# Funnel attention followed by a multiplicative FFN: early keys, queries and w3 transposed on TensorE instead of by DMA, weight loads spread between pairs, FFN work issued per matmul under a time budget

## The chip, the cores and the metric

The kernel runs on one core of one Trainium2 chip. The metric is the device time of one execution in microseconds (us). The span of a profiled run is about 1.8 us shorter than its time.

## The reference

```python
# q, k, v: (8 batches, 8 heads, 1152, 64); x: (4608, 512)
q_pool = q.reshape(B, H, S // 2, 2, D).mean(axis=3)              # 576 queries
scores = (1 / sqrt(D)) * q_pool @ k.T                            # 576 x 1152 per head
attn   = exp(scores - max) / sum
x      = (attn @ v) laid out as (B*576, 8*64)
a, b   = x @ w1, x @ w2                                          # 512 -> 1024
out    = ((a * b) @ w3) @ w_out                                  # 1024 -> 1024 -> 512
```

The kernel computes T = w3 @ w_out once, so that the last line is (a * b) @ T.

## The kernel before

The 64 heads are handled as 32 pairs of heads. For each pair a flat string of 9 key blocks x 576 queries = 5184 columns of scores runs through TensorE, and the strings of all pairs are cut into chunks of 512 columns, 324 in all. One iteration of the main loop handles two chunks: scores on TensorE into PSUM, the memory that takes its results (`psc`), the exponential on ScalarE into SBUF, the memory that its operands come from (`er`), the attention matmuls for what is ready (`po`, one accumulator for the whole pair), and FFN matmuls as filler so that TensorE does not stand while ScalarE works. There are 162 iterations, and 5184 / 1024 = 5.06 of them belong to a pair.

Scores need keys and queries transposed (`kT`, `qT`). Before, the DMA does this for every pair, and also for w3. `kst` (loaded keys) has 4 buffers, so the load for pair P + 4 waits until VectorE has copied the keys of pair P into `kc`.

```python
def prep(P):                                        # cut: the rows of the first two pairs
    kc = ab.tile([128, NJ, 2, D], FP16, tag="kc", bufs=2, name="kc")
    nc.vector.tensor_copy(out=kc..., in_=kst.pop(P))
    kT[P] = ab.tile([128, NJ, 128], FP16, tag="kT", bufs=3, name="kT")
    nc.sync.dma_start_transpose(out=kT[P], in_=kc.rearrange("p j u d -> p (j u d)"))
    ...                                             # qp = sum of neighbouring queries, VectorE
    qT[P] = ab.tile([128, NJ, 64], FP16, tag="qT", bufs=3, name="qT")
    nc.sync.dma_start_transpose(
        out=qT[P], in_=qps[pp][o:o + 64].rearrange("p c u d -> p (c u d)"))
    nc.vector.tensor_copy(out=vts[P % 4][:, :, :, 0:D], in_=vst.pop(P))

def scores(c):
    t = psum.tile([128, 2, CH], FP32, tag="psc", bufs=2, name="psc")
    ...                                             # matmuls: 64 rows, up to 512 columns
def expo(c):
    nc.scalar.activation(out=er[:, :, r:r + CH], in_=psc.pop(c), func=AF.Exp, ...)

def w3_transpose():                                 # once, at iteration 3
    for i in range(2):
        nc.sync.dma_start_transpose(out=w3T[:, 4 * i:4 * i + 4]..., in_=w3h[i]...)

def gen_ffn(t, tail):                               # filler: one yield = 4 matmuls of 512 columns
    ...
            pa = bank("pa", tail and ft % 2)
            for mc in range(NC):
                nc.tensor.matmul(pa, w1sb[...], xT[:, mc, t0:t0 + 512], ...)
            ...
            yield

load_k(0); load_q(0); load_v(0); prep(0)
load_k(1); load_q(1); load_v(1); prep(1)
load(2); load(3); load_w(); load_w12()
...
for it in range(NIT):
    if it == 3: w3_transpose()
    if it == 6: filler.append(gen_T())
    ...
    scores(2 * it);     expo(2 * it)
    scores(2 * it + 1); expo(2 * it + 1)
    if prepped < NP and it * 2 * CH >= (prepped - 2) * PAIR + 2 * CH:
        prep(prepped); prepped += 1                 # two pairs ahead of use
        if loaded < NP: load(loaded); loaded += 1
    credit = min(credit + 24 / 20.0, 2.4)           # filler pieces per iteration
    while (SQ * (nextJ + 1) - 1) // CH <= 2 * it - 1:
        attend(nextJ); nextJ += 1
        if nextJ % NJ == 0: fill(1)
    fill(3)
...                                                 # the last FFN units after the loop
```

The softmax here doesn't subtract the row's maximum and nothing guards it: scores larger than these inputs give would overflow.

Of the kernel before, what the change touches and what calls it, by code (L numbers as in the profile page):

```python
# [8 lines left out]
FP16 = mybir.dt.float16  # L9
AF = mybir.ActivationFunctionType  # L10
ALU = mybir.AluOpType
# [12 lines left out]
def kernel(  # L24
# [17 lines left out]
    NF = dff // 128  # L42
    NP = B * H // 2
    SCL = 16.0
    SCALE = 0.5 * float(D) ** -0.5

    const = ctx.enter_context(tc.tile_pool(name="const", bufs=1))
# [11 lines left out]
    wosb = const.tile([128, NF, dm], FP16)  # L59
    er = const.tile([128, 2, RING], FP16)  # L60
    vts = [const.tile([128, 2, NJ, VW], FP16, name=f"vt{i}") for i in range(4)]

    ctx.enter_context(tc.manual_schedule())

# [29 lines left out]
    def load(P):  # L94
        if P < NP:
            load_k(P)
            load_q(P)
            load_v(P)

    def prep(P):  # L100

        kc = ab.tile([128, NJ, 2, D], FP16, tag="kc", bufs=2, name="kc")
        nc.vector.tensor_copy(out=kc.rearrange("p j u d -> p u j d"), in_=kst.pop(P))  # L103
        kT[P] = ab.tile([128, NJ, 128], FP16, tag="kT", bufs=3, name="kT")
        nc.sync.dma_start_transpose(out=kT[P], in_=kc.rearrange("p j u d -> p (j u d)"))
        pp, o = P // 2, 64 * (P % 2)
        if P == 0:
            qps[pp] = ab.tile([128, NJ, 2, D], FP16, tag="qp", bufs=2, name="qp")
            rows = [slice(0, 64)]
        elif P == 1:  # L110
            rows = [slice(64, 128)]
        elif P % 2 == 0:
            qps[pp] = ab.tile([128, NJ, 2, D], FP16, tag="qp", bufs=2, name="qp")
            rows = [slice(0, 128)]
        else:
            rows = []
        for r in rows:
            src = qst[pp][r].rearrange("p u (c two) d -> p u c two d", two=2)
            nc.vector.tensor_tensor(
                out=qps[pp][r].rearrange("p c u d -> p u c d"),  # L120
                in0=src[:, :, :, 0, :], in1=src[:, :, :, 1, :], op=ALU.add)
        qT[P] = ab.tile([128, NJ, 64], FP16, tag="qT", bufs=3, name="qT")
        nc.sync.dma_start_transpose(
            out=qT[P], in_=qps[pp][o:o + 64].rearrange("p c u d -> p (c u d)"))
        nc.vector.tensor_copy(out=vts[P % 4][:, :, :, 0:D], in_=vst.pop(P))


    psc = {}
# [22 lines left out]

    po = {}

    def attend(J):

        P, j = divmod(J, NJ)
        if j == 0:
            po[P] = psum.tile([128, 2, 512], FP32, tag="po", bufs=1, name="po")
        r = (J * SQ) % RING
        for u in range(2):  # L160
            for i in range(5):
                f = 128 * i if i < 4 else SQ - 128
                nc.tensor.matmul(  # L163
                    po[P][:, u, VW * i:VW * i + D + 1],
                    er[:, u, r + f:r + f + 128],
                    vts[P % 4][:, u, j, 0:D + 1],
                    start=(j == 0 and i == 0), stop=(j == NJ - 1 and i == 4),
                    skip_group_check=True)
        if j < NJ - 1:
            return  # L170
        acc = po.pop(P)[:, :, 0:5 * VW].rearrange("p u (i w) -> p u i w", w=VW)
        rz = ab.tile([128, 2, 5, 1], FP32, tag="rz", bufs=2, name="rz")
        nc.vector.reciprocal(out=rz, in_=acc[:, :, :, D:D + 1])  # L173
        xn = ab.tile([128, 5, 2, D], FP16, tag="xn", bufs=3, name="xn")
        nc.vector.tensor_tensor(  # L175
            out=xn.rearrange("p i u d -> p u i d"), in0=acc[:, :, :, 0:D],
            in1=rz.to_broadcast([128, 2, 5, D]), op=ALU.mult)
        b, hp = divmod(P, 4)
        n0 = b * SQ
        nc.sync.dma_start_transpose(  # L180
            out=xT[:, hp, n0:n0 + 512].rearrange("p (i r) -> p i r", r=128),
            in_=xn[:, 0:4].rearrange("p i u d -> p (i u d)"))
        nc.sync.dma_start_transpose(
            out=xT[:, hp, n0 + 512:n0 + SQ].rearrange("p (i r) -> p i r", r=64),
            in_=xn[64:128, 4].rearrange("p u d -> p (u d)"))
# [1 line left out]

    w3h = []

    def load_w():  # L190
        for i in range(2):
            t = ffp.tile([128, 4, dff], FP16, tag="g", name="w3h")
            nc.gpsimd.dma_start(
                out=t, in_=moe_w3.rearrange("(c p) f -> p c f", p=128)[:, 4 * i:4 * i + 4])
            w3h.append(t)
        nc.gpsimd.dma_start(out=wosb, in_=moe_w_out.rearrange("(c p) f -> p c f", p=128))

    def load_w12():
        nc.gpsimd.dma_start(out=w1sb, in_=moe_w1.rearrange("(c p) f -> p c f", p=128))
        nc.gpsimd.dma_start(out=w2sb, in_=moe_w2.rearrange("(c p) f -> p c f", p=128))  # L200

    def w3_transpose():
        for i in range(2):
            nc.sync.dma_start_transpose(
                out=w3T[:, 4 * i:4 * i + 4].rearrange("p c a f -> p (c a) f"),
                in_=w3h[i].rearrange("p c f -> p (c f)"))

    def bank(pre, wide):
        if not wide:
            return psum.tile([128, 512], FP32, tag="ff", bufs=2, name=pre)  # L210
        return psum.tile([128, 2, 512], FP32, tag="psc", bufs=2, name=pre)[:, 0, :]

    def gen_T():

        for c in range(NF):
            pt = bank("pT", False)
            for a in range(NF):
                nc.tensor.matmul(pt, w3T[:, c, a, :], wosb[:, a, :],  # L218
                                 start=(a == 0), stop=(a == NF - 1))
                if a == 3:  # L220
                    yield
            nc.vector.tensor_copy(out=T16[:, c, :], in_=pt)
            yield

    def gen_ffn(t, tail):
        t0 = 512 * t
        gT = ffp.tile([128, NF, 512], FP16, tag="g", name="gT")
        for ft in range(NF):
            pa = bank("pa", tail and ft % 2)
            for mc in range(NC):  # L230
                nc.tensor.matmul(pa, w1sb[:, mc, ft * 128:ft * 128 + 128],  # L231
                                 xT[:, mc, t0:t0 + 512],
                                 start=(mc == 0), stop=(mc == NC - 1))
            asb = ffp.tile([128, 512], FP32, tag="asb", name="asb")
            if tail:
                nc.scalar.copy(out=asb, in_=pa)
            else:
                nc.vector.tensor_copy(out=asb, in_=pa)  # L238
            yield
            pb = bank("pb", tail and ft % 2)  # L240
            for mc in range(NC):
                nc.tensor.matmul(pb, w2sb[:, mc, ft * 128:ft * 128 + 128],  # L242
                                 xT[:, mc, t0:t0 + 512],
                                 start=(mc == 0), stop=(mc == NC - 1))
            nc.vector.tensor_mul(out=gT[:, ft, :], in0=pb, in1=asb)  # L245
            yield
        for i in range(4):
            pp = bank("pp", tail and i % 2)
            for ft in range(NF):
                nc.tensor.matmul(pp, gT[:, ft, 128 * i:128 * i + 128], T16[:, ft, :],  # L250
                                 start=(ft == 0), stop=(ft == NF - 1))
                if ft == 3:
                    yield
            osb = ffp.tile([128, dm], FP32, tag="osb", bufs=3, name="osb")
            if tail:
                nc.scalar.activation(out=osb, in_=pp, func=AF.Copy, bias=0.0,
# [4 lines left out]
            for s in range(2):  # L261
                b, f = divmod(t0 + 128 * i + 64 * s, SQ)
                rows = out[b * SQ:(b + 1) * SQ, :].rearrange("(p c) m -> c p m", c=NJ)
                nc.sync.dma_start(out=rows[f // 64], in_=osb[64 * s:64 * s + 64, :])
            yield


    NCHUNK = NP * PAIR // CH
    NIT = NCHUNK // 2

    load_k(0)
    load_q(0)
    load_v(0)
    prep(0)
    load_k(1)
    load_q(1)
    load_v(1)
    prep(1)
    load(2)
    load(3)  # L280
    load_w()
    load_w12()
    loaded, prepped = 4, 2

    filler = []
    n_units = NT // 512
    next_unit = 0
    T_started = False
    credit = 0.0
    nextJ = 0  # L290
    for it in range(NIT):
        if it == 3:
            w3_transpose()
        if it == 6:
            filler.append(gen_T())

        while next_unit < n_units:
            last_b = (512 * (next_unit + 1) - 1) // SQ
# [5 lines left out]
        expo(2 * it)  # L304
        scores(2 * it + 1)
        expo(2 * it + 1)

        if prepped < NP and it * 2 * CH >= (prepped - 2) * PAIR + 2 * CH:
            prep(prepped)
            prepped += 1  # L310
            if loaded < NP:
                load(loaded)
                loaded += 1
        credit = min(credit + 24 / 20.0, 2.4)

        def fill(n):
            nonlocal credit
            while n > 0 and filler and credit >= 1.0:
                try:
                    next(filler[0])  # L320
                    credit -= 1.0
                    n -= 1
                except StopIteration:
                    filler.pop(0)

        while (SQ * (nextJ + 1) - 1) // CH <= 2 * it - 1:
            attend(nextJ)
            nextJ += 1
            if nextJ % NJ == 0:
                fill(1)  # L330
        fill(3)
    while nextJ < NP * NJ:
        attend(nextJ)
        nextJ += 1
    for g in filler:
        for _ in g:
            pass
# [34 lines left out]
```

## Time and profile before

| | before |
|---|---|
| time, median of 4 runs | 497.48 us (496.44 to 498.61) |
| first exponential starts | 26.35 us |
| iterations 0 to 8 | 26.35 to 83.14 us |
| mean iteration, 40 to 150 | 2.37 us |
| last exponential ends | 447.0 us |
| after it (FFN left over, last store) | 49.9 us |

The iteration times are read from the trace: every second exponential on ScalarE starts an iteration. In the profile, L143 is the score matmul, L149 the exponential, L163 the attention matmul, L173 and L175 the normalization, L218 the matmul for T, and L231, L242 and L250 the FFN. PE is TensorE, PEld its weight load, ACT ScalarE, DVE VectorE, POOL GpSimd and SP SyncE.

First the page of before: the span, busy times, two of the rows in 40 slices (a digit is tenths busy), and the chain of work that ended last by engine.

```profile
span 496.9 us, 11617 instructions
...
PE 415.5 (84%) x4960; PEld 213.4 (43%) x4960; DVE 182.8 (37%) x313; ACT 327.2 (66%) x349; POOL 69.4 (14%) x105
...
PE   0062009987999999999999999999999999999996
...
ACT  1073006776877888888887778787777888882332
...
PE 69%; DMA 15%; ACT 7%; issue 5%; DVE 3%; POOL 1%; ACTq 0%; DVEq 0%; POOLq 0%
```

There are two stages. In the first six slices of 12.4 us TensorE is empty but for parts of the third and fourth; after that it is full. Nearly all of the DMA's 15% of the chain lies in the first stage. The waits of before say for what (engine, line, releaser: total us, times, longest us):

```profile
ACT er L149 <- PE psc L143: 132.8, 130, 32.0
...
PE psc L143 <- DMA qT<-qp: 32.3, 2, 25.7
...
PE pT L218 <- DMA w3T<-w3h: 28.5, 1, 28.5
...
PE psc L143 <- ACT er L149: 9.2, 25, 0.7
...
PE po L163 <- DVE xn L175: 4.9, 13, 1.2
```

TensorE stands 60.8 us for transposes done by DMA: 25.7 and 6.6 us for queries, 28.5 us for w3. The timeline of before shows them in place (start and duration in us; in brackets the idle time and what ended it), and below them one iteration of the full stage:

```profile
18.61 10.85 SPq L123 DMA_TRANSPOSE qT<-qp  x1
25.70 1.04 PE L143 MATMUL psc<-qT,kT 64*128 64x512 f16 x6 [25.70 <-DMA qT<-qp]
...
42.36 0.98 PE L143 MATMUL psc<-qT,kT 64*128 64x448 f16 x6 [6.56 <-DMA qT<-qp]
...
74.76 1.46 PE L218 MATMUL pT<-wosb,w3T 128*128 128x512 f16 x3 [28.48 <-DMA w3T<-w3h]
...
82.65 0.61 PE L143 MATMUL psc<-qT,kT 64*128 64x512 f16 x6
83.19 0.78 PE L163 MATMUL po<-vt_78,er 128*128 128x65 f16 x20
83.81 1.03 PE L218 MATMUL pT<-wosb,w3T 128*128 128x512 f16 x4
84.77 0.39 PE L143 MATMUL psc<-qT,kT 64*128 64x128 f16 x4
```

The table by stretches of before tells whether the DMA or its latency is the limit (stretch and length in us, busy of PE, PEld, DVE, ACT, POOL with counts, then granted TensorE clock, DMA share, GB/s):

```profile
20.00:40.00 20.00, 8.66 (x106) 5.11 (x107) 1.59 (x3) 9.48 (x10) 4.17 (x7) 1.00 1.20 202
40.00:60.00 20.00, 3.53 (x34) 1.94 (x33) 1.04 (x2) 3.77 (x4) 2.54 (x4) 0.50 1.14 195
...
200.00:300.00 100.00, 97.89 (x1253) 50.44 (x1252) 45.70 (x78) 81.37 (x86) 18.38 (x27) 1.00 1.02 146
```

While TensorE stands, the DMA moves 195 to 202 GB/s with its engines busy throughout (shares of 1.14 and 1.20). Between 200 and 300 us TensorE is busy 98%, with ScalarE at 81%.

### The profile page before, as it was taken

To read this page: it belongs to the slowest core of one execution; us is meant where nothing else is said; L and a number is where in the kernel's file an instruction comes from. 1 tells how busy PE (TensorE), PEld (TensorE's weight loads), DVE (VectorE), ACT (ScalarE), POOL (GpSimd) and SP (SyncE) were. 2 spreads that over 40 slices of the span, in tenths; PEclk is the share of its full clock that TensorE was granted. 3 is DMA by queue.
4 is the path that set the end of the run, shared out by engine and by line. 5 is a ranking of instruction groups with operands and counts; after the bars stand their busy time and mean duration, and the time that the engine had idled before them with its cause. 6 is when DMAs were issued, how large, how long until landed. Compare 5 with 4: busy or idle time off the path is not lost.

```text
span 496.9 us, 11617 instructions
## 1 busy us (share of the span) xinstructions
PE 415.5 (84%) x4960; PEld 213.4 (43%) x4960; DVE 182.8 (37%) x313; ACT 327.2 (66%) x349; POOL 69.4 (14%) x105
## 2 busy tenths in 40 slices
PE   0062009987999999999999999999999999999996
PEld 0031005444444545555555444444454545554442
DVE  1200001323453445355434543454355345424130
ACT  1073006776877888888887778787777888882332
POOL 6411101111111111112211111111110000000000
PEclk9996558998999999999999999999999999999998
DMA  8999999899899898999998989998999254012213
GB/s 129 200 203 189 202 202 167 125 119 137 100 129 136 162 155 136 159 143 154 124 176 147 121 124 187 139 133 116 160 177 109 66 92 99 15 45 65 55 31 86
DMA packets 117059, 64.73 MB, mean 130 GB/s; under 512 B 88848, under 2 KB 106256, under 8 KB 117008
## 3 DMA queue, kind: packets, MB, share of 16 engines
q0 software_dynamic: 25168, 33.56, 46.2%
q1 hardware_dynamic: 91840, 30.43, 39.8%
q8 instruction: 39, 0.64, 0.6%
q14 instruction: 12, 0.10, 0.1%
HBM read 67.11 MB, written 9.44 MB: 154 GB/s over the span
## 4 chain that ended last, share of the span: by engine, by line
PE 69%; DMA 15%; ACT 7%; issue 5%; DVE 3%; POOL 1%; ACTq 0%; DVEq 0%; POOLq 0%
PE po L163 18%; PE psc L143 16%; PE pa L231 11%; PE pb L242 11%; PE pp L250 10%; ACT er L149 7%; DMA w3T<-w3h 6%; DMA w3h<-in_moe_w_dram 4%; DMA kst<-in_k_dram 2%; PE pT L218 2%; DVE xn L175 2%; DMA qst<-in_q_dram 2%; DVE rz L173 1%; DMA xT<-xn 0%; POOL kst L83 0%
## 5 line engine op out<-in xcount | busy, mean ns | idle before, releaser
L149 ACT ACTIVATE er<-psc 128x1024 f16<-128x1024 f32 x324 | 311.8, 1023 | 133.2 <-PE psc L143 132.8
L143 PE MATMUL psc<-qT,kT 64*128 64x512 f16 (+7 forms) x1152 | 114.5, 291 | 42.9 <-DMA qT<-qp 32.3
L163 PEld LDWEIGHTS <-er 128*128 128x128 f16 x2880 | 98.5, 98 | 48.4 <-issue 35.5
L143 PEld LDWEIGHTS <-kT 64*128 64x128 f16 x1152 | 44.3, 95 | 125.3 <-issue 91.9
L231 PE MATMUL pa<-xT,w1sb 128*128 128x512 f16 x288 | 75.0, 382 | 0.3 <-DMA xT<-xn 0.3
L245 DVE TENSOR_TENSOR gT<-pb,asb 128x512 f16<-128x512 f32 x72 | 49.6, 689 | 68.4 <-PE pb L242 68.4
L242 PE MATMUL pb<-xT,w2sb 128*128 128x512 f16 x288 | 74.3, 380 | 0.0
L250 PE MATMUL pp<-T_73,gT 128*128 128x512 f16 x288 | 70.1, 379 | 0.0
L83 POOL DMA_DIRECT2D kst<-in_k_dram x32 | 23.2, 724 | 273.6 <-DVE kc L103 248.8
L238 DVE COPY asb<-pa 128x512 f32<-128x512 f32 x56 | 38.7, 691 | 57.8 <-PE pa L231 57.5
L218 PE MATMUL pT<-wosb,w3T 128*128 128x512 f16 x64 | 17.3, 400 | 28.5 <-DMA w3T<-w3h 28.5
L259 DVE TENSOR_SCALAR osb<-pp 128x512 f32<-128x512 f32 x28 | 19.3, 690 | 52.8 <-PE pp L250 52.8
L231 PEld LDWEIGHTS <-w1sb 128*128 128x128 f16 x288 | 25.4, 98 | 25.1 <-DMA xT<-xn 0.8
L242 PEld LDWEIGHTS <-w2sb 128*128 128x128 f16 x288 | 25.0, 98 | 23.0 <-issue 1.1
L250 PEld LDWEIGHTS <-gT 128*128 128x128 f16 x288 | 24.9, 97 | 22.9
L163 PE MATMUL po<-vt_77,er 128*128 128x65 f16 x720 | 31.2, 199 | 1.5 <-DVE xn L175 1.5
L163 PE MATMUL po<-vt_78,er 128*128 128x65 f16 x720 | 29.7, 194 | 0.9 <-DVE xn L175 0.9
L163 PE MATMUL po<-vt_80,er 128*128 128x65 f16 x720 | 29.4, 194 | 1.2 <-DVE xn L175 1.2
L163 PE MATMUL po<-vt_79,er 128*128 128x65 f16 x720 | 29.4, 194 | 1.2 <-DVE xn L175 1.2
L173 DVE RECIPROCAL rz<-po 128x10 f32<-128x10 f32 x32 | 7.1, 221 | 55.0 <-PE po L163 55.0
L175 DVE TENSOR_TENSOR xn<-po,rz 128x640 f16<-128x640 f32 x32 | 26.4, 824 | 1.1
L90 POOL DMA_DIRECT2D vst<-in_v_dram x32 | 23.7, 740 | 13.7 <-DMA wosb<-in_moe_w_out_dram 7.3
(24 smaller groups left out, 95.5 us busy)
## 6 DMA issues: line engine op xcount, KB each, us to landing
kst<-in_k_dram POOLq DMA_DIRECT2D x32, 288.0 KB, 4.9
qst<-in_q_dram POOLq DMA_DIRECT2D x32, 288.0 KB, 6.5
vst<-in_v_dram POOLq DMA_DIRECT2D x32, 288.0 KB, 8.8
out_dram<-osb SPq DMA_DIRECT2D x72, 128.0 KB, 3.9
w3h<-in_moe_w_dram POOLq DMA_DIRECT2D x2, 1024.0 KB, 20.0
wosb<-in_moe_w_out_dram POOLq DMA_DIRECT2D x1, 1024.0 KB, 27.1
w1sb<-in_moe_w_dram POOLq DMA_DIRECT2D x1, 1024.0 KB, 31.7
w2sb<-in_moe_w_dram POOLq DMA_DIRECT2D x1, 1024.0 KB, 35.2
```

What stands on the lines that cost most here:

```text
L83: nc.gpsimd.dma_start(out=kst[P].rearrange("p u j d -> p u (j d)"), in_=k[b, h0:h0 + 2].rearrange("u (p j) d -> p u (j d)", j=NJ))
L90: nc.gpsimd.dma_start(out=vst[P].rearrange("p u j d -> p u (j d)"), in_=v[b, h0:h0 + 2].rearrange("u (p j) d -> p u (j d)", j=NJ))
L143: nc.tensor.matmul(t[:, u, o:o + ln], kT[P][s, j, :], qv[s, f0:f0 + ln], start=True, stop=True)
L149: nc.scalar.activation(out=er[:, :, r:r + CH], in_=psc.pop(c), func=AF.Exp, bias=0.0, scale=SCALE)
L163: nc.tensor.matmul(po[P][:, u, VW * i:VW * i + D + 1], er[:, u, r + f:r + f + 128], vts[P % 4][:, u, j, 0:D + 1], start=(j == 0 and i == 0 ...
L175: nc.vector.tensor_tensor(out=xn.rearrange("p i u d -> p u i d"), in0=acc[:, :, :, 0:D], in1=rz.to_broadcast([128, 2, 5, D]), op=ALU.mult)
L218: nc.tensor.matmul(pt, w3T[:, c, a, :], wosb[:, a, :], start=(a == 0), stop=(a == NF - 1))
L231: nc.tensor.matmul(pa, w1sb[:, mc, ft * 128:ft * 128 + 128], xT[:, mc, t0:t0 + 512], start=(mc == 0), stop=(mc == NC - 1))
L238: nc.vector.tensor_copy(out=asb, in_=pa)
L242: nc.tensor.matmul(pb, w2sb[:, mc, ft * 128:ft * 128 + 128], xT[:, mc, t0:t0 + 512], start=(mc == 0), stop=(mc == NC - 1))
L245: nc.vector.tensor_mul(out=gT[:, ft, :], in0=pb, in1=asb)
L250: nc.tensor.matmul(pp, gT[:, ft, 128 * i:128 * i + 128], T16[:, ft, :], start=(ft == 0), stop=(ft == NF - 1))
```

## The change

The intent is to start ScalarE early and keep it fed. The keys and queries of pairs 0 to 5 (`NPE = 6`) and all of w3 are transposed on TensorE, through PSUM, in the order in which they are needed; loads of weights are placed between loads of pairs; and the filler is issued one matmul at a time until a running estimate of TensorE's time (`busy`) reaches a schedule (`due`) of 1.95, later 2.19 us per iteration. Attention is issued per block of 128 queries, not 576.

```diff
+    NPE = 6
+    T_AT = (9, 14)
+    T_MM, T_TR, T_SC, T_AV = 0.216, 0.06, 0.63, 0.061
+    PACE0, PACE1 = 1.95, 2.19
 ...
+    def prep_dma(P):            # as prep before: copy keys, add queries, two DMA transposes
+    def prep_pe(P):
+        new_kq(P)
+        pool_q(P)
+        kc = ab.tile([128, NJ, 2, D], FP16, tag="kc", bufs=2, name="kc")
+        nc.vector.tensor_copy(out=kc..., in_=kst.pop(P))
+        t1 = psum.tile([128, 1024], FP16, tag="ff", bufs=2, name="t1")
+        t2 = psum.tile([128, 1024], FP16, tag="ff", bufs=2, name="t2")
+        for c in range(NJ):
+            nc.tensor.transpose(t2[...], qps[pp][o:o + 64, c]..., ident[...])
+        for j in range(NJ):
+            nc.tensor.transpose(dst, kc[:, j]..., ident)
+        ...                      # three copies PSUM -> qT, kT, then the values
 ...
-    def w3_transpose():          # two DMA transposes
+    def w3_transpose(c):         # 8 TensorE transposes into one "ff" bank, one copy
 ...  gen_T, gen_ffn: one yield per matmul
-                if a == 3:
-                    yield
+                if a < NF - 1:
+                    yield T_MM, False
 ...
-    load(2)
-    load(3)
-    load_w()
-    load_w12()
+    load(1); load(2); load_w3(0); load_w(wosb, moe_w_out); load(3); load_w3(1)
+    waiting = [lambda: load(4), lambda: load_w(w1sb, moe_w1), lambda: load_w(w2sb, moe_w2),
+               lambda: load(5), lambda: load(6)]       # two of these after each preparation
 ...
+    def fill(until, settle=False):
+        while filler and (not whole if settle else busy < until):
+            cost, whole = next(filler[0])
+            busy += cost
 ...  in the loop
-        if prepped < NP and it * 2 * CH >= (prepped - 2) * PAIR + 2 * CH:
+        busy += T_SC
+        due = (due if filler else busy - T_SC) + (PACE0 if it < 20 else PACE1)
+        lead = 0.5 if prepped < NPE else 2.0
+        if prepped < NP and it * 2 * CH >= (prepped - lead) * PAIR + 2 * CH:
+            if prepped < NPE:
+                fill(0, settle=True)
             prep(prepped)
```

The rule for `lead`: a pair transposed on TensorE is prepared half a pair ahead of its use, a pair transposed by DMA two pairs ahead, and pairs are prepared in order.

## The prediction

> **What bounds the kernel now.** *Start, 0 to 79 us:* DMA (15% of the chain of waits). The first score matmul starts at 25.70 us, after waiting for the transposed queries; PE then waits 6.56 us for the next queries and 28.48 us for w3T (timeline, waits). ScalarE has then done 14 of 324 exponentials. The table by stretches shows DMA saturated at about 200 GB/s. *From 79 us:* TensorE, busy 97% at 160 to 400 us (ScalarE 83%).
>
> From starts in the timeline (82.65, 83.19, 83.81, 84.77 us): an iteration's two score chunks take 0.54 us, 20 attention matmuls 0.59, four 512-wide matmuls 0.86, switching about 0.1. So an iteration costs about 0.63 + 0.061 per block of two attention matmuls + 0.216 per FFN matmul. The 155 iterations from 79 to 449 us sum to about 340 us but took 370: the rest is iterations short of filler, where ScalarE (1.94 us for two exponentials) binds, an empty filler, and waits for the normalization (po has one buffer). Tail: 449 to 492 TensorE, then 5 us for eviction and store.
>
> **What the change does.** It removes DMA transposes for six pairs and w3, places weights between pairs, and fills TensorE time per matmul. It adds 108 + 64 TensorE transposes and their PSUM copies. The Trainium skill, "VectorE: DVE Perf Modes", section "The three transpose paths", gives 390 ns for a 128x128 TensorE transpose and 1309 ns by DMA; this trace has no TensorE transpose, and w3T's 64 blocks took 29.7 us to land. From the 65-column matmul's 29.5 ns pace I estimate 0.06 us each in a row: 6.5 + 3.8 us.
>
> **Sum.**
> - q0 and k0 land by about 8 us; add and copy (0.75 + 0.46), transposes, copies: first scores at 11.5 us.
> - Iterations 0 to 8 at ScalarE's pace, 9 x 1.95: 29 us. At 200 GB/s pairs 0 to 6 and all weights land by about 60 us, each ahead of need.
> - From there TensorE work: 153 x 0.63 + 1369 x 0.061 + 864 x 0.216 (FFN) + 17.7 (T with transposes) + 4 preparations x 1.08 = 389 us, to 418.
> - Last eviction and store 5: 423.
> - Losses: preparations of pairs 3 to 5 wait for VectorE and both FFN PSUM banks, outside the budget: about 7. Normalization waits, 32 x 0.3: about 9. Split runs and jitter: 2.
> - Total about **441 us**.
>
> Nearly all is on the critical path: about 45 us from the start, of which preparation gives back about 10, and 15 to 20 from smoother filling. The leftover of FFN unit 6 (0.45 unit) after the loop hides the 2.3 us xT wait at 448.7.
>
> Range 430 to 454 us. Faster by over 2%: 0.98; same 0.015; slower 0.005.
>
> **Right if:** first exponential near 12 us; 20 exponentials by 32 us; no TensorE idle over 3 us after 12 us; iterations near 2.2 to 2.3 us; loop ends near 385 us, then about 51 us of FFN; TensorE busy over 92%. A step is wrong if first scores wait on a load beyond 14 us, iterations exceed 2.4 us, or xn waits exceed 15 us on TensorE.
>
> **What would make it wrong:** TensorE transposes far slower than 0.06 us, or leaving the clock low (granted 0.5 in the first 40 us); VectorE, strictly in order, blocking on a late load of pair 6 or 7 and holding the FFN banks; preparation and filler colliding on PSUM banks for several us each.

## The result, and the profile after

| | before | after | predicted |
|---|---|---|---|
| time, median of 4 runs, us | 497.48 (496.44 to 498.61) | 463.37 (458.66 to 464.58) | 441 (430 to 454) |
| first exponential, us | 26.35 | 9.98 | near 12 |
| iteration 9 starts, us | 83.14 | 29.54 | about 29 |
| iteration 32 starts, us | 139.8 | 106.2 | |
| mean iteration 40 to 150, us | 2.37 | 2.32 | 2.2 to 2.3 |
| last exponential ends, us | 447.0 | 406.2 | near 385 |
| after it, us | 49.9 | 56.6 | 56 |

The ratio of after to before is 0.9296 (95% interval 0.9229 to 0.9364). Here and below a ratio is the mean time of one kernel's fast runs over that of the other's of the same rounds, so it is not quite the ratio of the medians that are quoted. The change is faster, by 34 us. The prediction's direction was right; its size was not, and the result lies outside its range.

In the profile of after, L185 is the score matmul, L191 the exponential, L204 attention, L214 and L216 the normalization, L263 the matmul for T, L276, L289 and L299 the FFN, L152 and L157 the query and key transposes, and L248 the w3 transposes. Its page, the same lines with the GB/s row:

```profile
span 462.8 us, 11974 instructions
...
PE 422.5 (91%) x5132; PEld 222.4 (48%) x5132; DVE 195.6 (42%) x340; ACT 329.8 (71%) x350; POOL 69.6 (15%) x107
...
PE   2868888839999999999999999999999999999995
...
ACT  3868646728888888888888888888888888813332
...
GB/s 135 209 192 208 208 205 84 147 137 115 122 123 201 154 138 117 165 182 137 145 141 171 133 127 177 172 111 142 183 138 52 53 120 38 15 58 47 77 15 91
...
PE 80%; DVE 9%; DMA 5%; ACT 3%; issue 2%; POOL 0%; ACTq 0%; POOLq 0%
```

The empty start has gone, but the ninth slice (93 to 104 us) is a hole: 3 tenths on TensorE, 2 on ScalarE. The seventh slice moves only 84 GB/s, where its neighbours before it move 205. The waits of after:

```profile
ACT er L191 <- PE psc L185: 79.6, 122, 9.1
...
PE psc L185 <- DMA qT<-qp: 8.7, 1, 8.7
...
PE po L204 <- DVE xn L216: 4.5, 11, 1.2
...
PE psc L185 <- ACT er L191: 3.6, 9, 0.7
```

Of 60.8 us of waiting for DMA transposes 8.7 are left, in one wait. The timeline of after shows the early start, one preparation on TensorE (that of pair 3, at iteration 14), and then what led to the wait:

```profile
9.33 1.03 PE L185 MATMUL psc<-qT,kT 64*128 64x512 f16 x6 [1.00 <-DVE vt_77 L128]
...
45.13 0.43 PE L152 MATMUL t_688<-ident,qp 64*128 64x64 f16 x9 [1.03 <-DVE qp L119]
...
45.75 0.62 PE L157 MATMUL t_687<-ident,kc 128*128 128x128 f16 x8 [0.18 <-DVE kc L148]
...
47.58 0.62 PE L248 MATMUL w3t<-ident,w3h 128*128 128x128 f16 x8 [0.61 <-DVE kT L162]
...
48.84 1.02 ACT L191 ACTIVATE er<-psc 128x1024 f16<-128x1024 f32 x1 [2.91 <-PE psc L185]
...
76.74 0.72 POOL L90 DMA_DIRECT2D kst<-in_k_dram  x1 [13.24 <-DVE kc L148]
...
80.19 1.26 SPq L136 DMA_TRANSPOSE kT<-kc  x1
80.34 0.72 POOL L90 DMA_DIRECT2D kst<-in_k_dram  x1 [0.56 <-DVE kc L135]
...
81.56 3.42 SPq L138 DMA_TRANSPOSE qT<-qp  x1
...
84.85 0.72 POOL L90 DMA_DIRECT2D kst<-in_k_dram  x1 [2.48 <-DVE kc L135]
...
99.73 0.71 PE L185 MATMUL psc<-qT,kT 64*128 64x128 f16 x6 [8.69 <-DMA qT<-qp]
```

The transposes themselves are cheap: eight of keys with their fill take 0.62 us, and they start 56 ns apart. The preparation as a whole is not: the exponential at 48.84 us had waited 2.91 us.

The wait at 99.73 us is for pair 6, the first pair that the DMA still transposes. Its queries were issued at 81.56 us and landed 18.1 us later; this is the longest single piece of the chain that ended last:

```profile
81.56 18.13 DMA qT<-qp
```

Beside it, three loads of keys start at 76.7, 80.3 and 84.9 us, each with the queries and values of its pair behind it: 3 x 0.885 = 2.65 MB (pairs 9, 10 and 11) issued within about 10 us. Each was released by a copy of keys (L148, L135) that belongs to the preparations of pairs 5, 6 and 7, which fall in iterations 24, 25 and 27. Pair 6's own lead would have had it prepared at iteration 22, but pairs are taken in order and pair 5, on TensorE, is only due at iteration 24. The table by stretches of after:

```profile
20.00:40.00 20.00, 14.59 (x245) 9.59 (x244) 8.23 (x17) 13.58 (x15) 3.52 (x5) 1.00 1.20 199
40.00:60.00 20.00, 16.07 (x226) 8.63 (x223) 7.48 (x14) 15.08 (x16) 4.79 (x7) 1.00 1.16 207
60.00:80.00 20.00, 16.89 (x241) 10.66 (x239) 10.02 (x21) 9.89 (x11) 4.08 (x6) 0.91 0.86 134
80.00:100.00 20.00, 11.18 (x145) 5.93 (x144) 5.77 (x11) 9.49 (x10) 4.06 (x6) 0.90 1.29 155
...
200.00:300.00 100.00, 98.53 (x1283) 51.32 (x1281) 47.84 (x81) 84.30 (x88) 17.87 (x27) 1.00 1.01 154
```

Where the time went, by iteration starts: after is 52.9 us ahead at iteration 7 (78.76 against 25.9), 33.6 at iteration 32, 40.8 at the end of the loop, and 34.1 at the end. So about 19 us of the start's gain is given back between iterations 7 and 32. The last loss is only a shift: after leaves 238 FFN matmuls for the time after the last scores, before 208, and 30 x 0.216 = 6.5 us.

Iterations of after over 2.77 us, before the steady stretch, are: 4, in which pair 1 is prepared (3.04), 6, 11 and 16 (2.99, 2.81, 2.97), the preparations 9, 14, 19 and 24 (5.32, 4.85, 6.88, 5.81), and 29 and 30 (11.03, 3.54), the wait for pair 6.

### The profile page after: what moved, and what is told of

The parts are those of the page before. It is cut to its first block, busy times and chain, and to the rows that moved or that the text cites. A ratio compares the mean times of both kernels' runs of the same rounds, so it can differ in the third digit from the quotient of the medians.

```text
span 462.8 us, 11974 instructions
## 1 busy us (share of the span) xinstructions
PE 422.5 (91%) x5132; PEld 222.4 (48%) x5132; DVE 195.6 (42%) x340; ACT 329.8 (71%) x350; POOL 69.6 (15%) x107
## 4 chain that ended last, share of the span: by engine, by line
PE 80%; DVE 9%; DMA 5%; ACT 3%; issue 2%; POOL 0%; ACTq 0%; POOLq 0%
PE po L204 22%; PE psc L185 20%; PE pp L299 12%; PE pa L276 12%; PE pb L289 11%; DVE xn L216 5%; DMA qT<-qp 4%; ACT er L191 2%; PE pT L263 2%; DVE rz L214 1%; DMA kst<-in_k_dram 1%; PE w3t L248 1%; DVE kT L162 1%; DVE qT L158 1%; DVE qp L119 0%
## 5 line engine op out<-in xcount | busy, mean ns | idle before, releaser
L191 ACT ACTIVATE er<-psc 128x1024 f16<-128x1024 f32 x324 | 313.4, 1021 | 83.6 <-PE psc L185 79.6
L204 PEld LDWEIGHTS <-er 128*128 128x128 f16 x2880 | 99.2, 98 | 55.3 <-issue 35.9
L185 PE MATMUL psc<-qT,kT 64*128 64x512 f16 (+7 forms) x1152 | 109.5, 291 | 15.0 <-DMA qT<-qp 8.7
L185 PEld LDWEIGHTS <-kT 64*128 64x128 f16 x1152 | 43.3, 95 | 88.3 <-issue 72.6
L289 PE MATMUL pb<-xT,w2sb 128*128 128x512 f16 x288 | 79.7, 379 | 0.7 <-DVE gT L294 0.7
L276 PE MATMUL pa<-xT,w1sb 128*128 128x512 f16 x288 | 80.0, 381 | 0.0
L299 PE MATMUL pp<-T_73,gT 128*128 128x512 f16 x288 | 70.1, 379 | 0.0
L289 PEld LDWEIGHTS <-w2sb 128*128 128x128 f16 x288 | 25.7, 97 | 24.1 <-issue 1.7
L299 PEld LDWEIGHTS <-gT 128*128 128x128 f16 x288 | 25.5, 97 | 24.5
L276 PEld LDWEIGHTS <-w1sb 128*128 128x128 f16 x288 | 25.8, 98 | 23.1 <-issue 0.3
L204 PE MATMUL po<-vt_78,er 128*128 128x65 f16 x720 | 30.6, 195 | 2.3 <-DVE xn L216 1.8
L204 PE MATMUL po<-vt_77,er 128*128 128x65 f16 x720 | 31.3, 197 | 1.0 <-DVE xn L216 0.6
L204 PE MATMUL po<-vt_79,er 128*128 128x65 f16 x720 | 30.1, 193 | 1.6 <-DVE xn L216 1.1
L204 PE MATMUL po<-vt_80,er 128*128 128x65 f16 x720 | 29.8, 194 | 1.2 <-DVE xn L216 0.9
L283 ACT COPY asb<-pa 128x512 f32<-128x512 f32 x16 | 9.4, 587 | 27.5 <-PE pa L276 27.5
L216 DVE TENSOR_TENSOR xn<-po,rz 128x640 f16<-128x640 f32 x32 | 26.4, 824 | 1.1
L214 DVE RECIPROCAL rz<-po 128x10 f32<-128x10 f32 x32 | 7.1, 221 | 33.5 <-PE po L204 33.5
```

The costliest lines, as they stand in the source:

```text
L185: nc.tensor.matmul(t[:, u, o:o + ln], kT[P][s, j, :], qv[s, f0:f0 + ln], start=True, stop=True)
L204: nc.tensor.matmul(po[P][:, u, VW * i:VW * i + D + 1], er[:, u, r:r + 128], vts[P % 4][:, u, j, 0:D + 1], start=(j == 0 and i == 0), stop= ...
L216: nc.vector.tensor_tensor(out=xn.rearrange("p i u d -> p u i d"), in0=acc[:, :, :, 0:D], in1=rz.to_broadcast([128, 2, 5, D]), op=ALU.mult)
L276: nc.tensor.matmul(pa, w1sb[:, mc, ft * 128:ft * 128 + 128], xT[:, mc, t0:t0 + 512], start=(mc == 0), stop=(mc == NC - 1))
L289: nc.tensor.matmul(pb, w2sb[:, mc, ft * 128:ft * 128 + 128], xT[:, mc, t0:t0 + 512], start=(mc == 0), stop=(mc == NC - 1))
L299: nc.tensor.matmul(pp, gT[:, ft, 128 * i:128 * i + 128], T16[:, ft, :], start=(ft == 0), stop=(ft == NF - 1))
```

## The experiments

My theory before them was that the miss has three parts: (1) the burst of loads beside pair 6's transposes, about 10 us; (2) TensorE preparations that stop scores while VectorE copies, outside the budget; (3) a steady iteration dearer than my sum. The rivals were: the DMA transposes are simply slow, whatever runs beside them; the preparations cost no more than predicted; and the filler's grain brought the 15 to 20 us I had given it, with the loss elsewhere.

Summary; each line's ratio is to the runs of before, so runs are compared by ratio.

| run | based on | median us | ratio (95%) |
|---|---|---|---|
| a0_after | after, repeated | 465.16 | 0.9341 (0.9312 to 0.9371) |
| e1_hold_loads | after | 461.09 | 0.9284 (0.9258 to 0.9309) |
| e2_prep6_early | after | 457.03 | 0.9193 (0.9170 to 0.9217) |
| e3_split_prep | after | 456.80 | 0.9179 (0.9161 to 0.9197) |
| e4_coarse_fill | after | 469.82 | 0.9459 (0.9439 to 0.9479) |
| e5_no_pe_pairs | after | 482.31 | 0.9698 (0.9681 to 0.9715) |
| e6_before_w3_pe | before | 482.44 | 0.9708 (0.9689 to 0.9727) |
| e7_order | after | 470.70 | 0.9456 (0.9426 to 0.9486) |
| e8_hold_but_q9 | e1 | 462.19 | 0.9301 (0.9282 to 0.9321) |
| e9_early_and_split | e2 + e3 | 457.32 | 0.9197 (0.9179 to 0.9216) |
| e10_prep_in_budget | e9 | 466.79 | 0.9343 (0.9303 to 0.9382) |
| e11_pace | e10 | 458.58 | 0.9116 (0.9075 to 0.9156) |
| e12_kc3 | e9 | 457.68 | 0.9211 (0.9191 to 0.9232) |
| e13_kc3_pace | e12 | 453.61 | 0.9136 (0.9109 to 0.9162) |
| e14_half_exp | after | 457.12 | 0.9189 (0.9170 to 0.9209) |
| e15_w12_later | e13 | 455.30 | 0.9152 (0.9126 to 0.9177) |
| e16_early_pace | e2 | 452.88 | 0.9115 (0.9072 to 0.9158) |

All gave correct results; about e14, which is wrong, see there.

### a0_after: the change once more

No edit.

> The changed kernel again, as the control of this batch. Both theories: 463 us, between 458 and 465, a ratio to before near 0.93. If its runs spread by over 4 us again, the theory that the wait for pair 6's queries depends on how the DMA traffic falls says that the spread is in that wait (8.7 us in the profiled run) and nowhere else.

465.16 us, ratio 0.9341; the wait for pair 6's queries was 8.3 us, and the first 44 iterations repeated within 0.12 us, but for 29 and 30 (10.64 and 3.75 us, before 11.03 and 3.54). The holes are the kernel's, not one run's. Its six runs spread by 4.8 us again; as one of them was profiled, the expectation about where the spread lies is not tested.

### e1_hold_loads: the loads of pairs 9 to 11 held back

```diff
             elif loaded < NP: ...
+            elif prepped in (7, 8):
+                held += 1
 ...
+                if J // NJ == 5:     # after pair 5's normalization, GpSimd first reads its rz
+                    nc.gpsimd.tensor_copy(out=gate, in_=last_rz[0]...)
+                    for _ in range(held): load(loaded); loaded += 1
```

> The loads of pairs 9 to 11 are held back until pair 5 is normalized, so they don't share the DMA with the transposes of pair 6. Theory A (contention: three preparations within 8 us free three buffers, and 2.65 MB of loads fall on the transposes): pair 6's query transpose lands in under 6 us instead of 18.1, the 8.7 us wait of TensorE goes, time 453 to 456 us (8 to 10 less). Rival B (the transposes are issued too late, 5 iterations before use, behind others in their queue): the wait stays over 5 us, time 460 or more.

Pairs 9 and 10 are held by the edit, pair 11 behind them in GpSimd's queue. Pair 6's keys landed 4.7 us after issue and its queries 4.0 us (13.1 and 18.1 us in after), and TensorE did not wait for them: iterations 27 to 31 took 2.1 to 2.5 us. The landing times of e1, keys (issued at 81.00 us), then queries (82.36 us):

```profile
DMA to landing us min/median/max: 4.7/4.7/4.7
...
DMA to landing us min/median/max: 4.0/4.0/4.0
```

That settles why the transposes were slow: not the transposes by themselves, but what moved beside them. The time fell by only 4.1 us (461.09 against 465.16), because iteration 33 now took 8.4 us. A line of the waits of e1 shows why:

```profile
DVE qp L119 <- DMA qst<-in_q_dram: 12.7, 3, 6.1
```

The queries of pairs 8 and 9 share one tile; the add for pair 8 waited 6.1 us, until 105.3 us, for pair 9's half, which I had held. VectorE ran nothing else meanwhile, and TensorE then stood 4.7 us for an FFN copy behind it. So the wait was moved, not removed. In the profiled run, the slowest of the six (464.88 us), iterations 24 and 25 also took 2.8 us longer than in the control, so this trace shows the repair and its price, but not the 4.1 us.

### e2_prep6_early: pair 6 prepared at iteration 22, ahead of pair 5

```diff
+        if it == 22:
+            new_kq(5)
+            prep_dma(6)
+        if prepped == 6:
+            prepped = 7
+            load(loaded); loaded += 1
```

> Pair 6 is prepared at iteration 22, before pair 5, in the stretch where the DMA runs empty (71 to 77 us in the changed kernel's profile). Theories A and B both: wait gone, 453 to 456 us. It tells them from rival C, that the wait is not on the critical path because TensorE work is fixed and filler makes it up: then 461 or more, with the same loop end.

457.03 us, 8.1 us under the control. There is no wait for pair 6's queries any more. Its transposes were no faster (keys 70.9 to 83.8 us, queries 72.2 to 92.1 us): freeing its `kst` buffer earlier also started the next load earlier. What helped is 9 us more of lead, not a quieter DMA. So the wait needs both, the burst and the short lead; taking either away removes it.

### e3_split_prep: the query add and key copy of a TensorE pair one iteration earlier

```diff
+    def stage_pe(P):             # pool_q(P), kc copy; called in the iteration before
     def prep_pe(P):
+        if P not in kcs: stage_pe(P)
 ...
+        if prepped < NPE and prepped not in kcs and \
+                (it + 1) * 2 * CH >= (prepped - lead) * PAIR + 2 * CH:
+            stage_pe(prepped)
```

> VectorE's query add and key copy for the pairs prepared on TensorE are issued one iteration earlier, nothing else. If TensorE's wait for VectorE before the transposes (about 1.3 us in each of four preparations at iterations 9, 14, 19, 24) is a true cost: 458 to 460 us, 3 to 5 less than the control. If preparation is bound by the copies out of PSUM afterwards or by ScalarE: within 1 us of the control. The wait for pair 6's queries stays in either case.

456.80 us with one slow run of 462.77, 8.1 us under the control by the ratios, more than I expected. Iterations 14, 19 and 24 went from 4.73 to 3.43, 6.88 to 4.82 and 5.81 to 4.51 us: 4.7 us. Theory (2) holds for this part: the wait for VectorE inside a preparation was on the critical path. Iteration 9 did not change (5.29 us). The other part came indirectly: pair 6's wait fell from 8.3 to 3.2 us, probably because the key copies freed `kst` buffers earlier; no run isolates that.

### e4_coarse_fill: filler in runs of four matmuls

```diff
-                cost, whole = next(filler[0])
-                busy += cost
+                for _ in range(4):
+                    cost, whole = next(filler[0])
+                    busy += cost
+                    if whole: break
```

> The changed kernel with its filler taken four matmuls at a time (as the kernel before does), the budget kept. My prediction gave the finer filling 15 to 20 us: then 478 to 485 us. The theory from the two traces (118 iterations of the steady stretch took 280.3 us before and 273.3 after, with 8 filler matmuls, 1.7 us, fewer): 5 to 7 us at most, so 466 to 471, mean iteration from 32 on 2.33 to 2.37 us against 2.31.

Ratio 0.9459 against 0.9341 of the control: 0.0118 x 497 = 5.9 us. The mean iteration 40 to 150 was 2.37 us, as in before, against 2.32. So the fine grain brings about 6 us, not the 15 to 20 that the prediction gave to "smoother filling".

### e5_no_pe_pairs: all pairs transposed by DMA

```diff
-    NPE = 6
+    NPE = 0                      # so every lead is two pairs; the first two pairs keep half-tile adds
```

> The changed kernel with all pairs' keys and queries transposed by DMA again; w3 still on TensorE, weights still placed between pairs. Theory A (the early DMA transposes are slow because they share the DMA with the loads): first exponential after 18 us, more waits of TensorE for transposes at pairs 1 to 3, 12 to 25 us of waits for DMA before 80 us, against about 14 us of preparation saved: 468 to 480 us. Rival (the weights' placement alone frees the DMA enough): no waits over 3 us after the first exponential, 450 to 463.

Ratio 0.9698, 0.0357 x 497 = 17.7 us worse than the control. The first exponential started at 28.07 us. A line of the waits of e5:

```profile
PE psc L185 <- DMA qT<-qp: 46.5, 4, 27.4
```

The transposes on TensorE are thus worth 17.7 us in place of the 37.8 us of waiting (46.5 - 8.7) that they save; by this sum of two traces the rest is paid back, above all by the four preparations, which cost 13.7 us over plain iterations.

### e6_before_w3_pe: the kernel before, with only w3 on TensorE

```diff
-    def w3_transpose():          # two DMA transposes at iteration 3
+    def w3_transpose(c):         # 8 TensorE transposes, one copy, issued inside gen_T
```

> The kernel before with w3 alone transposed on TensorE. If the 28.5 us wait for w3T is a true cost: T starts at 45 to 47 us, 466 to 474 us in all (23 to 31 less). If the DMA is so full that the pairs' loads then bind in its place: 480 to 490, with new waits for kT and qT of pairs 3 and 4 of over 8 us.

482.44 us, ratio 0.9708: 14.5 us gained, of 28.5 us that TensorE had stood for w3. I expected 466 to 474. Three lines of its waits:

```profile
PE psc L145 <- DMA qT<-qp: 39.5, 4, 25.6
...
PEld L145 <- DMA kT<-kc: 23.7, 3, 20.5
...
DVE kc L105 <- DMA kT<-kc: 5.8, 1, 5.8
```

The wait for queries, 32.3 us in two waits before, is 39.5 us in four: iteration 6 fell from 33.9 to 6.4 us, but iterations 14 and 15 rose to 7.9 and 5.5. Half of what the one wait gave went into later waits for the DMA, which was busy throughout until 80 us (shares of 1.15 to 1.20). This looks like the pattern in after: without its first stall the loop reaches pairs whose data the DMA has not brought yet.

### e7_order: all weights in one block after pair 3

```diff
     load(1); load(2)
-    load_w3(0); load_w(wosb, moe_w_out)
     load(3)
-    load_w3(1)
+    load_w3(0); load_w3(1); load_w(wosb, ...); load_w(w1sb, ...); load_w(w2sb, ...)
-    waiting = [load(4), w1, w2, load(5), load(6)]
+    waiting = [load(4), load(5), load(6)]
```

> The changed kernel with the weights loaded in one block after pair 3, as in the kernel before. If their placement between pairs matters: T's first matmul waits for w_out, 3 to 6 us at iterations 9 to 11, and pair 4's load comes after all weights, so preparation at iteration 19 or 24 waits: 466 to 472 us. If not: 460 to 465, as the control.

Ratio 0.9456: 0.0115 x 497 = 5.7 us worse than the control. Iteration 9 took 10.2 us, of which 4.5 us were TensorE's wait for w_out. The placing of the loads is worth about 6 us. Its profiled run was the fastest of six (466.47 us, median 470.70), and in it the wait for pair 6's queries was only 2.3 us.

### e8_hold_but_q9: as e1, but pair 9's queries not held

```diff
+                if prepped == 7: load_q(9)
 ...
-                    for _ in range(held): load(loaded); loaded += 1
+                    load_k(9); load_v(9); load(10); loaded = 11
```

> The held loads again, but with the queries of pair 9 loaded at their old place, since pair 8's query add reads both pairs' tile and VectorE stood 6.1 us before it at iteration 33 when they were held. If that was the only thing that ate the gain: iterations 27 to 40 all near 2.3 us, 453 to 456 us (ratio to before 0.912 to 0.918). If holding loads costs by itself: another wait of over 4 us for a load between iterations 31 and 40, 459 or more.

462.19 us, no better than e1. Iterations 27 to 39 were clean, but iteration 40 took 9.2 us, with a wait of 4.8 us for pair 8's queries: the held loads now fell beside pair 8's transposes.

### e9_early_and_split: e2 and e3 together

The edits of e2 and e3.

> Both repairs: pair 6 prepared at iteration 22, and VectorE's part one iteration early. The split alone cut iterations 14, 19 and 24 by 4.7 us together and the wait for pair 6's queries from 8.3 to 3.2 us; what is left of it, with its second slow iteration, is about 4.6 us. So 452 to 453 us by the median (ratio 0.908 to 0.912), if the two overlap as told; 447 or less if they add in full; 456 or more if the early preparation's own VectorE work undoes the split.

457.32 us: the two gains of about 8 us do not add at all. A line of its waits:

```profile
DVE kc L136 <- DMA kT<-kc: 7.0, 1, 7.0
```

VectorE, which works in order, stood 7.0 us for a `kc` buffer that pair 6's slow key transpose was still reading, and iterations 28 and 29 took 6.8 and 3.5 us.

### e10_prep_in_budget: e9, a preparation charged to the budget

```diff
             prep(prepped)
+            if prepped < NPE:
+                busy += 18 * T_TR + 1.0
```

> As the run before, and each preparation on TensorE is charged 2.08 us in the filler budget, so that less filler follows it. If TensorE's waits of 0.6 to 0.8 us for the PSUM copies after a preparation come from filler that follows at once: iterations 9, 14, 19, 24 shrink by over 1 us each, 2 to 4 us less than the run before in all. If TensorE work is merely moved to the tail: within 1 us, with the loop 6 to 8 us shorter and the tail as much longer.

466.79 us with two slow runs among them; ratio of the fast ones 0.9343. A miss. Iteration 9 fell to 3.0 us and 14 to 2.8, but 24 rose to 6.5, and 34 took 6.4 with new waits for the DMA. The FFN work that the loop had skipped came after it (64.6 us there, not 56.6), and the last exponential came no sooner. That the loop only reached the DMA's limit earlier is argued.

### e11_pace: e10 with a longer schedule step

```diff
-    PACE0, PACE1 = 1.95, 2.19
+    PACE0, PACE1 = 1.95, 2.27
```

> As the run before, with a pace of 2.27 us in place of 2.19 from iteration 20. Score chunks waited for their PSUM buffer (ScalarE) in iterations of 4 filler matmuls (2.05 us), 5.4 us in 118 iterations; with 5 matmuls nearly always it should vanish: mean iteration from 40 on about 2.37 us with more filler in it, 3 to 5 us less in all. If the loop merely takes filler from the tail: within 1.5 us.

Inconclusive. Three runs, the profiled one among them, were slow at 461 to 463 us; the three fast ones were 450.33, 454.01 and 455.95. The ratio 0.9116 rests on those three.

### e12_kc3: e9 with a third kc buffer

```diff
-        kc = ab.tile([...], tag="kc", bufs=2, name="kc")
+        kc = ab.tile([...], tag="kc", bufs=3, name="kc")
```

> Both repairs (pair 6 early, VectorE's part one iteration early) with three buffers for the key copy in place of two. If VectorE's 7.0 us stand before pair 7's copy is what ate the second gain: iterations 28 and 29 at 2.3 us, 450 to 453 us. If the DMA then holds back something else in the same stretch: a new wait of over 3 us between iterations 27 and 41, 455 or more.

457.68 us, unchanged. VectorE no longer stood, but a wait of 4.6 us for pair 6's queries was back, and iterations 29 and 30 took 6.9 and 4.2 us.

### e13_kc3_pace: e12 with the schedule step at 2.24

```diff
-    PACE0, PACE1 = 1.95, 2.19
+    PACE0, PACE1 = 1.95, 2.24
```

> As the run before with a pace of 2.24 us from iteration 20. If score chunks wait for ScalarE in the short iterations (2.05 us, 4 filler matmuls): 2 to 4 us less than the run before. If the loop only takes work from the tail: within 1 us.

453.61 us, 4.1 us under e12. 33 FFN matmuls moved into the loop (205 are left after the last scores, not 238). The last exponential started only 1.9 us later (400.14 against 398.20). Part of that is an earlier start of iteration 32; in iterations 40 to 149 alone, 25 more FFN matmuls took 2.84 us, 0.11 us each, while outside the loop each costs 0.216 us. So the steady loop still had TensorE time to give: it was not bound by the sum of TensorE's work alone, as my model had it.

### e14_half_exp: exponential of half the columns only

```diff
+    nc.vector.memset(er[:, 0], 1.0)
+    nc.vector.memset(er[:, 1], 1.0)
-        ... out=er[:, :, r:r + CH], in_=psc.pop(c) ...
+        ... out=er[:, :, r:r + CH // 2], in_=psc.pop(c)[:, :, 0:CH // 2] ...
```

This kernel leaves out half of the exponentials. It passed the comparison only because these inputs give scores so small that their exponentials are near 1.

> The changed kernel with exponentials of half the columns (wrong results on purpose; the rest of their output is set to 1 once). ScalarE is then at about 55% of its work. If the steady iteration's excess is the wait for ScalarE: mean iteration from 40 to 150 falls from 2.315 to 2.26 to 2.28 us, and the waits inside score chunks go. If it is TensorE's own cost (pieces, weight loads): it stays at 2.30 to 2.32.

The mean iteration 40 to 150 fell from 2.317 to 2.275 us, though TensorE's work was the same. The time from the first to the last score matmul of a chunk pair fell from 0.361 to 0.316 us per iteration. From iteration 32 to the last exponential it was 6.2 us faster in all. The starts in the traces show the release itself: in 67 of 110 iterations of after (40 to 149) the first score matmul of the second chunk began 50 to 80 ns after the end of the exponential that frees its `psc` buffer; in e14 it never began less than 690 ns after. So ScalarE, releasing `psc` late, costs about 0.04 us of each iteration even at 98% TensorE busy.

### e15_w12_later: e13 with w1 and w2 loaded after pair 7

```diff
-    waiting = [load(4), w1, w2, load(5), load(6)]
+    waiting = [load(4), load(5), load(6), load(7), w1, w2]
```

> As the run with three copy buffers and a pace of 2.24, and w1 and w2 loaded after pair 7. If the early waits are a matter of order: no iteration over 4 us after 25, iteration 32 starts before 92 us (94.8 and more so far), 446 to 450 us. If the DMA can't supply the pairs at this pace: a wait of over 3 us for kT, qT or a load stays between iterations 25 and 41, 452 to 456.

455.30 us; I expected 446 to 450. A wait of 6.4 us for pair 6's queries (iteration 29: 8.9 us) came with the DMA nearly empty soon after, at 95 to 100 us (6 GB/s). So the volume up to 100 us is not the limit. That the order within the burst is, is argued, and the order that I tried did not help.

### e16_early_pace: e2 with the schedule step at 2.24

```diff
 # the edit of e2_prep6_early, and
-    PACE0, PACE1 = 1.95, 2.19
+    PACE0, PACE1 = 1.95, 2.24
```

> Pair 6 early as in the earlier run (457.0 us, no wait for its queries) and a pace of 2.24 us, nothing else. If the pace's gain (about 4 us between the two runs with three copy buffers) comes from fewer waits of score chunks for ScalarE and a shorter tail: 452 to 454 us. If it came from the early stretch there: 456 to 458.

452.88 us, ratio 0.9115 to before. It beats both kernels: by 44.4 us the kernel before on its own chip and, by the ratios, by about 9 to 11 us the change. TensorE did not wait for any DMA in its scores, and iterations 27 to 40 took 2.3 us on average. Two of its six runs took 457.0 us, against 450 to 453 in the others; they left no trace. Its page and its stretch from 80 to 100 us, where after had 11.18 us of TensorE work:

```profile
span 448.8 us, 11966 instructions
...
PE 418.3 (93%) x5132; PEld 222.0 (49%) x5132; DVE 195.7 (44%) x340; ACT 329.7 (73%) x350; POOL 69.9 (16%) x107
```

```profile
80.00:100.00 20.00, 19.74 (x256) 10.23 (x252) 10.17 (x18) 16.64 (x18) 4.08 (x6) 1.00 1.39 142
```

Against e2, 33 FFN matmuls moved into the loop, the last exponential started 1.5 us later, and the time after it fell by 6.6 us. In iterations 40 to 149 each of 25 more FFN matmuls cost 0.08 us.

## Why the prediction was right or wrong

**Right: the start, in part by luck.** First scores were predicted at 11.5 us and came at 9.33; iteration 9 was predicted at about 29 us and started at 29.54; the 20th exponential began at 30.4. The match at iteration 9 is two errors that cancel: the start was 2 us early, and iterations 0 to 8 took 2.17 us each, not 1.95. The cost of a TensorE transpose, estimated at 0.06 us in a row, was 0.056; where the granted clock was 0.5 (61.7 to 65.0 us), it was 0.107. The Trainium skill, "TensorE: Matmul & The Clock Gate", section "Part 4: PE-mode transpose", gives about 390 ns for one alone and about 275 ns within a kernel; this trace's single records are 220 ns long, but they overlap, and the pace at the full granted clock is 56 ns. For a sum of a row of them the pace is the number to use.

**Right: the normalization waits and the end.** 0.3 us per pair was predicted; the trace gives 0.063 us per iteration x 5.06 = 0.32, taken from the steps from an FFN matmul to the attention that a normalization delays, less one matmul. The time after the loop was 51.9 + 4.7 us, predicted about 51 + 5.

**Wrong, the largest: "At 200 GB/s pairs 0 to 6 and all weights land by about 60 us, each ahead of need", with "no TensorE idle over 3 us after 12 us".** The loads were about as told: pair 6's landed by 64 us and w2 by 55. I counted when loads land, not when pair 6's DMA transposes are issued. They were issued at iteration 25 because of pair 5, with five iterations to go, and landed 13.1 and 18.1 us later beside three loads. Iterations 29 and 30 took 14.57 us, about 10 us more than two plain ones. e1 shows that the loads beside them made the transposes slow (4.7 and 4.0 us without), and e2 that lead removes the wait (8.1 us gained). The Trainium skill, "Advanced Engine Details and Errata", section "X-Bar Transpose (TRN2)", says that transpose DMAs are as fast as regular ones. For the keys this holds here: a plain load of 0.29 MB of keys landed in 4.2 us ahead of the burst (issued at 76.74 us) and in 11.9 and 13.2 us within it, and the transpose of as many keys in 4.7 us nearly alone (e1) and 13.1 us in the burst. So what I missed is not a slow kind of transfer but a full DMA; only the queries, half as many bytes and issued behind the keys by SyncE, took longer still (18.1 us). What agrees with the burst is "DMA: Bandwidth & Descriptors", section "Issuing engines are not separate DMA queues": transfers of all issuing engines run on the same 16 DMA engines and interleave. My list of what would make it wrong named VectorE "blocking on a late load of pair 6 or 7"; the pair was right, but it was TensorE that waited, for a transpose.

**Mis-sized: the preparations.** The sum gave them 4 x 1.08 = 4.3 us and "about 7" for waits, 11.3 in all. Measured, iterations 9, 14, 19 and 24 took 22.86 us, 13.7 more than four of 2.3: 2.4 us short. The mechanism was the predicted one: e3 shows the wait for VectorE, 4.7 us of it in three of the four. What the rest is made of no run isolates.

**Wrong: "an iteration costs about 0.63 + 0.061 per block of two attention matmuls + 0.216 per FFN matmul", taken as a bound by TensorE alone.** With 8.89 blocks, 4.72 FFN matmuls and the 0.07 us of predicted losses the model gives 2.263 us; measured 2.317. Over 130 iterations this is 7 us. The 0.63 came from one iteration. The term includes a wait that I had left out: scores waiting for ScalarE to release `psc`. e14 shows 0.04 us of it per iteration, and e13 and e16 show the same from the other side: FFN matmuls added to the loop cost 0.11 and 0.08 us each, not 0.216.

**Wrong: "15 to 20 from smoother filling".** e4 gives about 6 us. I had set the 370 us of before's loop against a sum of 340 that used the same 0.63 and so had blamed the filler for time that ScalarE takes. In before the stretch from the first to the last score matmul per iteration was 0.434 us, 0.405 in e4, 0.361 in after; finer filling shortens it but does not remove it.

**Not predicted, small:** iterations 6, 11 and 16, in which ScalarE sets the pace and a normalization falls, took 2.8 to 3.0 us; I put 2 to 4 us on them, which is argued from the trace only.

The parts, 10 + 7 + 2.4 + about 3, are 22 us; the miss of the profiled run was 464.6 - 441 = 24. About 2 us stay without a cause.

The parts of the change, each by its run: TensorE pairs 17.7 us (e5), fine filler 5.9 (e4), load order 5.7 (e7), and w3 alone, on the kernel before, 14.5 (e6). They sum to 44, more than the 34 gained. That they overlap because each frees time that another wait for the DMA partly takes is what e6 suggests.

**Open:** why the repairs don't add. In e8, e9, e10, e12 and e15 a wait reappeared where transposes of pairs 6 to 8 met loads. That the place moves is shown; a rule that tells beforehand where it lands is not.

## What to carry to other kernels

When a stall is taken away from the start, ask what the loop will reach sooner and whether its data will be there; in a chain of staged preparations compute for each item the iteration at which it is really issued, since an item with a long lead behind one with a short lead loses its lead. A transfer's time has to be costed together with the loads that the same step releases. Before adding up an engine's work as the bound, test the marginal cost of one more piece: if it is far below the piece's own time, the engine still waits for another one somewhere.

## What the Trainium skill lacked or had wrong

- "TensorE: Matmul & The Clock Gate", section "Part 4: PE-mode transpose", and "VectorE: DVE Perf Modes", section "The three transpose paths", give the latency of one TensorE transpose (390 ns, or about 275 ns in a kernel) and do not say what pace a row of them keeps; the first page gives paces for rows of matmuls (section "Back-to-back issue gap"), not of transposes. Here 128x128 fp16 transposes in a row start 56 ns apart, with a granted clock of 1.00 in the stretches around (20 to 60 us), and 107 ns apart at 62 to 64 us, where the granted clock was 0.50.
- "Advanced Engine Details and Errata", section "X-Bar Transpose (TRN2)", calls transpose DMAs as fast as regular DMAs, which the keys here bear out. It lacks what a burst does to both: 4.7 us to land a transpose of 0.29 MB nearly alone (e1), but 13.1 us for these keys, 18.1 us for the queries behind them and 11.9 to 13.2 us for plain loads of keys, when three loads of 0.885 MB move together.
- "TensorEngine Tiling (Array Packing)", section "Key Properties", says that switching the tiling mode drains TensorE, without a cost. Here the step from a 128-row FFN matmul to a 64-row score matmul took 312 ns start to start, where FFN matmuls among themselves take 216 ns: 96 ns. The way back, to the attention matmuls, cost about 93 ns. The second occurs in every iteration, the first in 90 of 110. No run tells the switch apart from the other differences between these matmuls.
